# A banded Toeplitz matrix built on VectorE instead of by way of DRAM, and two input loads not tied to slots

## The chip, the cores and the metric

One core of one Trainium2 chip. The metric is the device time of one execution in microseconds (us). Medians of an execution series are given; where single executions matter they are listed. The record of each execution also holds the mean clock granted to TensorE.

## The reference, cut to what matters

A causal depthwise convolution with 7 taps per head, the taps normalised by a softmax, is followed by an RWKV channel mix:

```python
# x: (8, 4160, 192) float32; weight: (8 heads, 7 taps)
w = softmax(weight, axis=-1)
y[b, s, h, :] = sum_k w[h, k] * x_padded[b, s + k, h, :]      # 6 zeros in front
xk = mu_k * y + (1 - mu_k) * y_prev;  xr = mu_r * y + (1 - mu_r) * y_prev
k = relu(xk @ w_k);  v = (k * k) @ w_v;  r = sigmoid(xr @ w_r)
out = r * v
```

## The kernel before: the parts concerned

The convolution runs on TensorE (PE). Blocks of 128 rows of x are multiplied by a 128x128 banded "Toe" matrix per head, which yields 120 new rows. x comes in 18 groups of blocks; three buffers hold them. The first four groups are transposed on PE; the others go through DRAM (`y_write`, then a transposing DMA load `y_read`). Group numbers below are the code's (what the recorded texts call groups 5 and 6 are numbers 4 and 5); "conv 4" is the convolution of group 4.

```python
def x_tile(g, eng):
    xb = three.tile([P, GB, 2, D], BF16, tag="xb", name="xb")
    if blk0 == 0:
        eng.memset(xb[0:32, 0, :, :], 0.0)
    elif g > 3:
        eng.memset(xb[0:1, 0, 0, 0:2], 0.0)      # ties the load to this point of VectorE's queue
    if blk0 + nb == NBLK:
        eng.memset(xb[:, nb - 1, :, :], 0.0)
...
def load_toe():        # w_row: the taps, zero-padded, written to DRAM as w_scr before this
    nc.gpsimd.dma_start(out=toe, in_=bass.AP(tensor=w_scr.tensor, offset=w_scr.offset + K - 1,
                                             ap=[[H * P - 1, P], [P, H], [1, P]]))
...
def y_read(g):         # issued on SyncE's queue (SP)
    nc.sync.dma_start_transpose(out=yTs[p][:, :, YC + r0 : YC + r1], in_=y_drams[p][r0:r1, :])
...
def warm(n):           # filler: keeps PE busy so that its clock rises
    ps = psV.tile([P, BANK], FP32, tag="v", name="warm")
    for _ in range(n):
        nc.tensor.matmul(out=ps, lhsT=ones_t, rhs=zeros, start=True, stop=True)
...
# prologue, in order
load_x(0); warm(WARM); softmax()
nc.sync.dma_start(out=w_scr, in_=w_row); load_toe()
load_x(1); load_wk(); load_x(2); load_wr(); load_wv()
# convolution of group 0, warm(2), transposes, warm(5), convolution of group 1, warm(3), x_tile(3), load_x(3), main loop
```

## Time and profile before

| | kernel before |
|---|---|
| time, median (range) | 458.6 us (458.35 to 459.82), 3 executions |
| span of the profiled execution | 456.8 us |
| PE busy | 444.2 us, 97% |
| first convolution matmul | 11.77 us |
| first convolution matmul of group 4 | 36.67 us, behind a wait of 1.62 us for data |
| PE idle, 0 to 50 us / 50 to 400 us | 8.4 us / 0 us |

The prediction shows the lines.

### The profile page before, as it was taken

The numbers are of one execution on the slowest core, as the hardware profiler recorded it, in microseconds if no ns is written. First come the engines' busy times: TensorE is split into PE (matmuls) and PEld (weight loads), VectorE is DVE, ScalarE is ACT, GpSimd is POOL, SyncE is SP. The second block draws the span as 40 slices with busy tenths as digits, with TensorE's granted clock in tenths as the row PEclk, the third lists the DMA queues.
The fourth block names the chain that finished last, engine by engine and source line by source line (L and its number), as shares of the span: only waits on it lengthen the run. The fifth ranks groups of instructions, "written<-read, shape, count | busy, mean of one in ns | idle before, by whom it ended". The sixth has DMA issues, their size and how long they took to land.

```text
span 456.8 us, 10049 instructions
## 1 busy us (share of the span) xinstructions
PE 444.2 (97%) x3958; PEld 303.3 (66%) x3958; DVE 383.0 (84%) x759; ACT 355.8 (78%) x464; POOL 48.7 (11%) x69
## 2 busy tenths in 40 slices
PE   8877999999999999999999999999999999999996
PEld 3544676676777667767767677667676676666676
DVE  2598789887998888897998998987998997988963
ACT  2677987888888688888888788888887877767771
POOL 5742001102030010101020010100200000000000
PEclk9999999999999999999999999999999999999999
DMA  4999696899679794955859695778655563411223
GB/s 75 164 104 201 127 234 137 148 193 184 160 144 188 194 151 123 155 137 143 158 128 186 154 193 126 132 133 189 118 135 152 140 151 95 108 63 60 71 70 96
DMA packets 134402, 64.18 MB, mean 141 GB/s; under 512 B 85747, under 2 KB 133907, under 8 KB 134355
## 3 DMA queue, kind: packets, MB, share of 16 engines
q1 hardware_dynamic: 96050, 48.60, 42.7%
q0 software_dynamic: 38304, 14.95, 28.9%
q8 instruction: 31, 0.51, 0.4%
q14 instruction: 17, 0.13, 0.1%
HBM read 29.65 MB, written 37.25 MB: 146 GB/s over the span
## 4 chain that ended last, share of the span: by engine, by line
PE 94%; DVE 2%; DMA 2%; ACT 1%; issue 1%; POOL 0%; DVEq 0%
PE ps_k L348 39%; PE ps_v L454 37%; PE ps_r L431 5%; PE ps_r L432 5%; PE ps_c L205 4%; PE warm L556 3%; DMA xb<-in_x_dram 2%; PE ps_k L374 1%; DVE yT L274 1%; DVE xr L329 0%; PE ps_t L263 0%; DVE xr L326 0%; DVE k L405 0%; DVE d L287 0%; ACT r_sb L438 0%
## 5 line engine op out<-in xcount | busy, mean ns | idle before, releaser
L386 ACT ACTIVATE k_sb<-ps_k 128x1024 bf16<-128x1024 f32 x260 | 248.2, 1025 | 56.4 <-PE ps_k L348 52.2
L348 PE MATMUL ps_k<-xk,wk 128*128 128x512 bf16 (+3 forms) x1056 | 199.3, 374 | 0.5 <-ACT k_sb L386 0.4
L454 PE MATMUL ps_v<-wv,k 128*128 128x192 bf16 x2048 | 195.0, 246 | 1.9 <-DVE k L405 1.0
L454 PEld LDWEIGHTS <-k 128*128 128x128 bf16 x2048 | 172.8, 98 | 25.8 <-DVE k L405 1.2
L405 DVE TENSOR_TENSOR k<-k_sb 128x1024 bf16<-128x1024 bf16 x256 | 172.4, 684 | 4.5 <-ACT k_sb L386 4.3
L348 PEld LDWEIGHTS <-wk 128*128 128x128 bf16 (+1 forms) x1056 | 63.0, 96 | 104.7 <-issue 72.8
L467 DVE TENSOR_TENSOR o_sb<-ps_v,r_sb 128x384 f32<-128x384 f32 x128 | 70.9, 554 | 43.5 <-PE ps_v L454 42.8
L438 ACT ACTIVATE r_sb<-ps_r 128x768 bf16<-128x768 f32 x64 | 52.8, 825 | 15.9 <-PE ps_r L432 13.8
L225 ACT CAST y<-ps_c 120x480 bf16<-120x480 f32 (+5 forms) x85 | 39.7, 527 | 16.1 <-PE ps_c L205 16.1
L112 POOL DMA_DIRECT2D xb<-in_x_dram x36 | 32.5, 908 | 154.2 <-PE ps_k L348 67.5
L431 PE MATMUL ps_r<-wr,xr 128*128 128x192 bf16 x256 | 47.5, 246 | 1.2 <-DVE xr L329 1.0
L432 PE MATMUL ps_r<-wr,xr 128*128 128x192 bf16 x256 | 47.4, 246 | 0.3 <-DVE xr L329 0.3
L329 DVE TENSOR_TENSOR xr<-xr,yT 128x1024 bf16<-128x1024 bf16 (+1 forms) x66 | 36.3, 549 | 2.3
L329 DVE TENSOR_TENSOR xk<-xk,yT 128x1024 bf16<-128x1024 bf16 (+1 forms) x66 | 36.2, 549 | 2.3
L205 PE MATMUL ps_c<-xb,toe 128*128 128x480 bf16 (+4 forms) x144 | 31.8, 321 | 1.9 <-DMA xb<-in_x_dram 1.6
L287 DVE TENSOR_TENSOR d<-yT 128x1536 bf16<-128x1536 bf16 (+2 forms) x37 | 31.6, 853 | 1.5 <-DMA yT<-y_dram 1.5
L326 DVE TENSOR_SCALAR xk<-d,mu 128x1024 bf16<-128x1024 bf16 (+1 forms) x66 | 27.6, 418 | 0.2
L326 DVE TENSOR_SCALAR xr<-d,mu 128x1024 bf16<-128x1024 bf16 (+1 forms) x66 | 27.4, 414 | 0.0
L432 PEld LDWEIGHTS <-xr 128*128 128x128 bf16 x256 | 25.0, 98 | 2.3 <-issue 1.7
L431 PEld LDWEIGHTS <-xr 128*128 128x128 bf16 x256 | 25.0, 98 | 1.8 <-DVE xr L329 1.2
L228 ACT CAST y<-ps_c 120x480 bf16<-120x480 f32 (+7 forms) x47 | 21.5, 509 | 0.8 <-DVE yT L233 0.6
L556 PE MATMUL warm<-zeros,ones_t 128*128 128x512 bf16 x46 | 13.2, 446 | 1.9 <-DVE zeros L565 1.4
(51 smaller groups left out, 84.0 us busy)
## 6 DMA issues: line engine op xcount, KB each, us to landing
out_dram<-o_sb SPq DMA_DIRECT2D x128, 192.0 KB, 2.5
y_dram<-y SPq DMA_DIRECT2D x10, 900.0 KB, 6.7
xb<-in_x_dram POOLq DMA_DIRECT2D x14, 480.0 KB, 7.9
xb<-in_x_dram POOLq DMA_DIRECT2D x6, 432.0 KB, 9.7
xb<-in_x_dram POOLq DMA_DIRECT2D x10, 192.0 KB, 5.0
y_dram<-y SPq DMA_DIRECT2D x3, 450.0 KB, 4.1
y_dram<-y SPq DMA_DIRECT2D x1, 810.0 KB, 6.4
xb<-in_x_dram POOLq DMA_DIRECT2D x2, 384.0 KB, 9.8
```

What stands on the lines that cost most here:

```text
L205: nc.tensor.matmul(out=ps[:, :, :, i * G : (i + 1) * G], lhsT=toe[:, h, :], rhs=xbs[g][:, :nb, :, h * G : (h + 1) * G], start=True, stop=True,
L225: copy(out=yh[:, :, :, c0 : c0 + n], in_=ps[:BLK, :, :, 0:n])
L326: nc.vector.tensor_scalar(out=o, in0=d[:, sl, :L], scalar1=mu[:, i, part : part + 1], scalar2=None, op0=ALU.mult)
L329: nc.vector.tensor_tensor(out=o, in0=o, in1=yT[:, sl, c0 : c0 + L], op=ALU.add)
L348: nc.tensor.matmul(out=ps[:, i, f * L : (f + 1) * L], lhsT=wk[r, 0 if hi else 1, fs], rhs=xk[r, i if hi else 2, :L], start=start and f == ...
L386: nc.scalar.activation(out=k_sb, in_=ps.rearrange("p a b -> p (a b)"), func=AF.Relu)
L405: nc.vector.tensor_tensor(out=o, in0=i, in1=i, op=ALU.mult)
L431: nc.tensor.matmul(out=o, lhsT=hi, rhs=wr[:, 0, :], start=True, stop=False)
L432: nc.tensor.matmul(out=o, lhsT=lo, rhs=wlo, start=False, stop=True)
L438: nc.scalar.activation(out=r_sb, in_=ps[:, :, 0 : 2 * D], func=AF.Sigmoid)
L454: nc.tensor.matmul(out=o, lhsT=k2[:, f, t * P : (t + 1) * P], rhs=wv[:, f, :], start=(f == 0), stop=(f == NF - 1),)
L467: nc.vector.tensor_tensor(out=o_sb[:, :n, :], in0=v_ps.pop(m)[:, :n, :], in1=r_sbs.pop(m)[:, :n, :], op=ALU.mult)
```

## The change

The intent: the Toe matrix no longer goes to DRAM and back. Along a row it is periodic with period 8 inside its band, so VectorE makes it as (pattern of period 8) x (band mask). `mod8` is a mask of "column mod 8 equals row mod 8", made from the identity; `w_all` is the product of taps and shifted masks; a sum over the taps gives the pattern `w_per`; two masked products write `toe`. The matrix being ready sooner, 16 of the 36 warm-up matmuls go. Second part: groups 4 and 5 lose the small memset that tied their loads to a slot.

```diff
-    WARM = 36
+    WARM = 20
...
-        elif g > 3:
+        elif g > 5:
             eng.memset(xb[0:1, 0, 0, 0:2], 0.0)
...
-    def load_toe(): ...
+    def masks_mod8():                       # twice, into the halves of mod8
+        nc.vector.tensor_reduce(out=mod8[:, 8 * i : 8 * i + 8],
+            in_=ident.rearrange("p (c r) -> p r c", r=8), axis=mybir.AxisListType.X, op=ALU.add)
+    def masks_band(): ...                   # two affine_selects on GpSimd
+    def make_toe():
+        nc.vector.tensor_tensor(out=w_all, in0=w_nrm.unsqueeze(3).to_broadcast([P, H, K, 8]),
+            in1=bass.AP(tensor=m.tensor, offset=m.offset, ap=[m.ap[0], [0, H], [1, K], [1, 8]]), op=ALU.mult)
+        nc.vector.tensor_reduce(out=w_per, in_=w_all.rearrange("p h k r -> p h r k"),
+            axis=mybir.AxisListType.X, op=ALU.add)
+        for h0, h1 in ((0, 3), (3, H)):
+            nc.vector.tensor_tensor(out=toe[:, h0:h1, :] ..., in0=w_per ..., in1=band ..., op=ALU.mult)
...
         nc.vector.memset(ones_t, 1.0)
+        x_tile(0, nc.vector)
         nc.vector.memset(zeros, 0.0)
... (ident now ahead of load_x(0), the band mask after it)
         softmax()
-        nc.sync.dma_start(out=w_scr, in_=w_row)
-        load_toe()
+        make_toe()
         load_x(1)
```

More of the change, by code (lines that the diff above doesn't have):

```diff
@@ L129 @@
     ident = const.tile([P, P], BF16)
-    w_row = const.tile([P, H, P], BF16)
-    w_scr = dram.tile([P, H, P], BF16)
+    w_nrm = const.tile([P, H, K], FP32)
+    mod8 = const.tile([P, 16], FP32)
+    w_all = const.tile([P, H, K, 8], FP32)
+    w_per = const.tile([P, H, 8], BF16)
+    band = const.tile([P, P], BF16)
     toe = const.tile([P, H, P], BF16)
@@ L169, in softmax @@
         nc.vector.tensor_tensor(
-            out=w_row[:, :, 0:K],
-            in0=w_exp[:, :, ::-1],
+            out=w_nrm,
+            in0=w_exp,
             in1=w_sum.unsqueeze(2).to_broadcast([P, H, K]),
@@ L174, in softmax, with masks_band @@
         )
-    def load_toe():
-        nc.gpsimd.dma_start(
-            out=toe,
-            in_=bass.AP(
-                tensor=w_scr.tensor,
-                offset=w_scr.offset + K - 1,
-                ap=[[H * P - 1, P], [P, H], [1, P]],
-            ),
-        )
+    def masks_mod8():
+        for i in range(2):
+            nc.vector.tensor_reduce(
+                out=mod8[:, 8 * i : 8 * i + 8],
+                in_=ident.rearrange("p (c r) -> p r c", r=8),
+                axis=mybir.AxisListType.X,
+                op=ALU.add,
+            )
+    def masks_band():
+        nc.gpsimd.affine_select(
+            out=band, in_=ones_t, pattern=[[-1, P]], compare_op=ALU.is_ge, fill=0.0, base=0, channel_multiplier=1
+        )
+        nc.gpsimd.affine_select(
+            out=band, in_=band, pattern=[[1, P]], compare_op=ALU.is_ge, fill=0.0, base=K - 1, channel_multiplier=-1
+        )
+    def make_toe():
+        m = mod8[:, :]
+        nc.vector.tensor_tensor(
+            out=w_all,
+            in0=w_nrm.unsqueeze(3).to_broadcast([P, H, K, 8]),
+            in1=bass.AP(tensor=m.tensor, offset=m.offset, ap=[m.ap[0], [0, H], [1, K], [1, 8]]),
+            op=ALU.mult,
+        )
+        with nc.allow_low_precision(reason="a sum of one number and zeros"):
+            nc.vector.tensor_reduce(
+                out=w_per,
+                in_=w_all.rearrange("p h k r -> p h r k"),
+                axis=mybir.AxisListType.X,
+                op=ALU.add,
+            )
+        for h0, h1 in ((0, 3), (3, H)):
+            n = h1 - h0
+            nc.vector.tensor_tensor(
+                out=toe[:, h0:h1, :].rearrange("p h (c r) -> p h c r", r=8),
+                in0=w_per[:, h0:h1, :].unsqueeze(2).to_broadcast([P, n, P // 8, 8]),
+                in1=band.rearrange("p (c r) -> p c r", r=8).unsqueeze(1).to_broadcast([P, n, P // 8, 8]),
+                op=ALU.mult,
+            )
     ys, yTs, y_drams = {}, {}, {}
@@ L564, in prologue @@
         nc.vector.memset(ones_t, 1.0)
+        x_tile(0, nc.vector)
         nc.vector.memset(zeros, 0.0)
-        x_tile(0, nc.vector)
-        x_tile(1, nc.vector)
-        x_tile(2, nc.vector)
-        nc.vector.memset(w_row, 0.0)
-        nc.vector.memset(wr[:, 2:4, :], 0.0)
-        load_x(0)
         nc.gpsimd.affine_select(
@@ L580, in prologue @@
         )
+        load_x(0)
+        masks_band()
         warm(WARM)
+        x_tile(1, nc.vector)
+        x_tile(2, nc.vector)
+        masks_mod8()
+        nc.vector.memset(wr[:, 2:4, :], 0.0)
         softmax()
-        nc.sync.dma_start(out=w_scr, in_=w_row)
-        load_toe()
+        make_toe()
         load_x(1)
```

## The prediction

> **What bounds the kernel now.** I read the page first, for the budget of each engine:
>
> ```profile
> span 456.8 us, 10049 instructions
> ...
> PE 444.2 (97%) x3958; PEld 303.3 (66%) x3958; DVE 383.0 (84%) x759; ACT 355.8 (78%) x464; POOL 48.7 (11%) x69
> ```
>
> PE idles for only 456.8 - 444.2 = 12.6 us, so a change that leaves the matmuls of the main loop alone must take its gain from those idle pieces, or from PE work that is there only to pass the time (the warm-up matmuls). The sums over stretches say where the idle is:
>
> ```profile
> 0.00:12.00 12.00, 10.61 (x40) 4.43 (x41) 2.38 (x10) 3.02 (x4) 6.88 (x16) 1.00 0.47 75
> 12.00:22.00 10.00, 8.64 (x87) 5.71 (x85) 5.58 (x14) 6.36 (x16) 7.80 (x13) 1.00 1.36 172
> 22.00:50.00 28.00, 22.33 (x181) 13.26 (x180) 25.92 (x55) 22.23 (x33) 7.93 (x10) 1.00 1.12 141
> 50.00:100.00 50.00, 50.00 (x439) 33.52 (x436) 41.60 (x81) 41.89 (x57) 3.77 (x4) 1.00 0.86 172
> ```
>
> The columns are the stretch and its length, then busy time of PE, PEld, DVE, ACT, POOL. From 50 us on PE is full, and the same view has 100.00 of 100.00 up to 400 us. Between 22 and 50 us PE misses 5.67 us, and DVE is the full engine (25.92 of 28). The change can therefore act only before 50 us; whatever the start gains there, the PE-bound rest passes on one for one. The chain of work that ended last, in order of time, names the two large early pieces:
>
> ```profile
> 1.39 10.54 PE warm L556 x36
> ...
> 11.94 0.39 PE ps_c L205 x6
> ...
> 28.86 7.68 DMA xb<-in_x_dram
> 36.54 0.14 issue
> 36.67 0.56 PE ps_c L205 x2
> ```
>
> The first is filler, so I ask the timeline what it fills for:
>
> ```profile
> 5.28 0.22 DVE L169 TENSOR_TENSOR w_row<-w_exp,w_sum 128x56 bf16<-128x56 f32 x1
> 5.53 0.33 SPq L584 DMA_DIRECT2D w_scr<-w_row  x1
> ...
> 6.81 4.63 PEld L556 LDWEIGHTS <-ones_t 128*128 128x128 bf16 x22 [0.19 <-issue]
> ...
> 8.34 0.59 POOL L177 DMA_DIRECT2D toe<-w_scr  x1 [3.39 <-DMA w_scr<-w_row]
> 8.93 1.49 POOL L112 DMA_DIRECT2D xb<-in_x_dram  x2
> ...
> 11.59 0.66 PEld L205 LDWEIGHTS <-toe 128*128 128x128 bf16 x8
> 11.77 0.66 PE L205 MATMUL ps_c<-xb,toe 128*128 128x144 bf16 x8
> ```
>
> The taps are ready at 5.28 + 0.22 = 5.50. The Toe matrix goes to DRAM and back: 2.5 us to land, then an issue at 8.34 that lands 3.2 us later, 11.54. Its first weight load is at 11.59, while the last warm-up matmul ends at about 11.77. So 36 matmuls were tuned to the round trip; filler and round trip end together, and removing only one of them gains almost nothing. POOL also stands behind the round trip: the loads of x group 1 wait for it until 8.93.
>
> **What the Trainium skill says.** "DMA: Bandwidth & Descriptors", section "Anatomy of one DMA — SWDGE (gpsimd) path", gives a transfer a fixed part of about 2.0 us. The trace agrees: 2.5 and 3.2 us for the two legs. "TensorE: Matmul & The Clock Gate", Part 1, says that the cold array runs at half clock, that the release depends on a free-running window of activity and not on a number of matmuls, and that an N=512 matmul then takes about 216 ns instead of 427. The trace agrees: weight loads of the warm-up stand 0.43 apart up to 6.47, and from 6.81 on 22 take 4.63 us (21 steps of 0.216); the granted-clock column says 1.00 throughout, so it doesn't show this. "VectorE: DVE Perf Modes", section "The TRN2 errata", gives (N+151)/0.96 ns for an fp32 tensor_tensor, and its perf-mode tier table one element per cycle for tensor_reduce, two for a bf16 tensor_tensor. For the 56-element multiply above the formula gives 216 ns, the trace 0.22; for the bf16 128x1024 square (512+151)/0.96 = 691, the page 684.
>
> **The change part by part.**
>
> Removed on the start path: the two DMA legs, and 16 warm-up matmuls. All 16 are warm ones: 16 x 0.216 = 3.46 us. But the zeros that the warm-up reads are now set after the x tile's memset, which takes a pitch of about 0.26 us, so PE begins at 1.65 instead of 1.39. If the clock rises at the same absolute time, about 6.72 (part way through the matmul that begins at 6.47), (6.72 - 1.65)/0.427 = 11.9 matmuls run cold, the other 8.1 take 1.75, and the warm-up ends at 8.47. If it rises 0.26 later, 8.73. Against 11.77 that is 3.0 to 3.3 us; I take 3.2.
>
> Added on DVE after 5.50: w_all, 448 fp32 elements, (448+151)/0.96 = 0.62; w_per, a reduction of 448 elements, 0.62; the masked product for heads 0 to 2, 384 bf16 elements, 0.36 at two per cycle (0.56 at one); for the other five, 640 elements, 0.49 (0.82). With some 0.03 between, the first heads are ready at 7.2 and all at 7.7 (7.4 and 8.3 if the broadcast pattern falls to one per cycle). Both are before 8.47, so this lies beside the warm-up. Ahead of the softmax DVE gets two 128-element reductions, 0.29 each, after the identity mask; they and the other memset end by about 2.8, and the softmax can't begin before the weights land at 4.0 (the first DVE reduction starts at 4.02). Hidden. On POOL ident moves ahead of the x loads and the band adds two selects of 0.31 (ident's duration) after them: band by about 5.1, used at about 6.8. Hidden too. x group 0 landed at 7.4 before and its issues move by about -0.1: in time for 8.5.
>
> Moved: loads of x group 1 are issued at about 5.15 instead of 8.93, 3.8 us earlier, and everything in POOL's queue behind them (first weights, x group 2, the second layer's weights, x group 3) likewise. Since PE moves by 3.2, the loads keep up. What follows conv 0 (casts, transposes, five more warm-ups) is a chain of latencies that I carry over unchanged.
>
> The second part: the two L94 memsets that tie the loads of groups 5 and 6 to the DVE queue (group numbers 4 and 5 in the code) go. Now look at the load of the first of them:
>
> ```profile
> 27.30 0.06 DVE L94 MEMSET xb<- 1x1 uint32 x2
> 27.39 0.22 DVE L96 MEMSET xb<- 128x192 uint32 x1
> ...
> 27.92 1.89 POOL L112 DMA_DIRECT2D xb<-in_x_dram  x2 [6.51 <-PE ps_k L348]
> ...
> 36.67 0.56 PE L205 MATMUL ps_c<-xb,toe 128*128 128x480 bf16 x2 [1.62 <-DMA xb<-in_x_dram]
> ...
> 37.59 0.53 DVE L274 COPY yT<-ps_t 128x720 bf16<-128x720 bf16 x1 [1.63 <-PE ps_t L263]
> ```
>
> POOL sat idle for 6.51 us; the wait is put down to PE, but the issue follows the DVE memset. The buffer itself (that of group 1) was free when conv 1 ended at about 16.9. Freed, this load follows x group 3 directly, at about 21.4 - 3.8 = 17.6. Behind group 3, which landed at about 26.5, it needs some 5.1 us (its second half landed 2.5 us after the first), so it lands near 26.5 - 3.5 + 5.1 = 28. PE wants it at (36.67 - 1.62) - 3.2 = 31.9. The wait vanishes with almost 4 us to spare: PE gets 1.62 us back and DVE, the full engine of this stage, its 1.63; I count them once, 1.6, and 0.1 for the memsets. For the other group, the last of its pair of sequences, the memset L96 stays on DVE, so its load remains tied. That costs nothing: its convolution comes at slot 14, after 50 us, and the load used to land by 43.
>
> Sum: 3.2 + 1.6 + 0.1 = 4.9. 458.6 - 4.9 = 453.7 us, 1.1% less.
>
> **The rivals.** (a) The front becomes bound by loads. x group 2 landed at about 19.6 and conv 2 began at 19.69: no slack there. If the earlier loads, now running beside the tail of group 0, win only 2.5 us and not 3.8, the start gains 2.5 and the time is 454.4. For it: the DMA engines run without a break from 10 to 26 us. Against it: between 8 and 10 us they are at 0.12, so there is idle time for the loads to move into. (b) DVE becomes the bound: the product reads a broadcast operand and slows to one per cycle or worse, and the Toe matrix is ready only at 9.5. Then the start gains 2.3: 454.6. Against it: even the slow estimate, 8.3, is under the warm-up's end. (c) The wait for group 4's data goes, but DVE, at 1.97 of each 2 us from 24 to 34, is replaced by another wait: the gain is the front alone, 455.4. Against it: DVE itself was idle in that wait. (d) The shorter warm-up ends before the clock is up, or PE cools again. 20 matmuls last 6.8 us by the estimate and the clock needed 5.3; run by run the moment moves. If all 20 ran cold, they would end at 1.65 + 8.54 = 10.2 and the gain be 1.7 less: 455.4.
>
> **Range and chances.** The rivals together lose at most about 3 us and I see hardly a mechanism for more than 1 us extra (a stall in 22 to 34 us that shrinks). So 452.4 to 455.8. Faster by over 2% means under 449.4, which would need 9.2 us out of an early stage that has 8.4 us of PE idle and 3.5 us of removed filler: 2%. Slower by over 2%: 1%. Within 2%: 97%.
>
> **What would show it.** Right: first conv matmul at 8.4 to 8.8 straight behind the warm-up; Toe products done by 7.7; first load of x group 1 issued near 5.2; load of group 4 issued at 17 to 19 and no DMA wait of PE near 32; PE full from about 45 us on. Wrong: an idle PE between warm-up and first convolution (Toe or x late), a wait of conv 1, of the first layer or of conv 2 for a load, DVE idle with another releaser between 20 and 45 us, or matmuls of 427 ns after 8 us.

## The result, and the profile after

454.68 us median (454.34 to 455.03, 4 executions) against 458.86 (458.35 to 459.82, 4 executions): ratio 0.9906, 95% interval 0.9887 to 0.9926. Ratios here are the mean time of one kernel's fast runs over that of the other's of the same rounds, so not quite the ratio of the medians quoted. The class is "same" (within 2%), the predicted 453.7 is 1.0 us low, and the range 452.4 to 455.8 holds. The profiled execution has a span of 453.3 us, 3.5 less than before.

The sums over the same stretches as in the prediction, for the changed kernel (stretch, length, busy PE, PEld, DVE, ACT, POOL):

```profile
0.00:12.00 12.00, 9.06 (x41) 4.00 (x42) 6.25 (x20) 4.08 (x7) 10.01 (x21) 1.00 0.82 93
12.00:22.00 10.00, 8.73 (x90) 6.12 (x89) 7.44 (x18) 7.68 (x15) 6.62 (x9) 1.00 1.31 148
22.00:50.00 28.00, 25.50 (x203) 15.37 (x202) 26.14 (x52) 24.82 (x40) 5.96 (x8) 1.00 1.12 159
50.00:100.00 50.00, 48.68 (x429) 32.88 (x428) 41.34 (x81) 40.53 (x53) 3.77 (x4) 1.00 0.92 168
```

Between 22 and 50 us PE has 25.50 instead of 22.33 us of work: the stage runs better. But from 50 to 100 us, where PE was full, it now misses 1.32 us. The timeline of the changed kernel, at the start and around conv 4:

```profile
6.41 0.95 DVE L206 TENSOR_REDUCE w_per<-w_all 128x64 bf16<-128x448 f32 x1
7.47 0.76 DVE L214 TENSOR_TENSOR toe<-w_per,band 128x384 bf16<-128x384 bf16 x2
8.25 0.68 PEld L240 LDWEIGHTS <-toe 128*128 128x128 bf16 x8
8.45 0.66 PE L240 MATMUL ps_c<-xb,toe 128*128 128x144 bf16 x8
...
24.72 0.57 PE L240 MATMUL ps_c<-xb,toe 128*128 128x240 bf16 x4 [0.81 <-DMA xb<-in_x_dram]
...
31.31 0.57 PE L240 MATMUL ps_c<-xb,toe 128*128 128x480 bf16 x2
```

The first convolution is at 8.45, 3.32 us earlier. Conv 4 is at 31.31, 5.36 us earlier and without its wait. A wait of 0.81 us at conv 3 is new. It does no lasting harm: the next convolution, 26.75 here and 30.24 before, is 3.49 earlier. So 5.36 us were won by 31 us, and 3.5 are left at the end. The chain of work that ended last, in order of time, names the place; the pieces from 40 to 60 us of the changed kernel:

```profile
43.25 6.68 DMA y_dram<-y
49.94 0.02 issue
49.95 7.71 DMA yT<-y_dram
57.67 0.02 issue
57.69 0.96 DVE d L322
```

This is the round trip of group 4's convolution result: written to DRAM, read back by the transposing load, then used by VectorE. The write begins 5.24 us earlier than before (48.49), but the load lands at 57.66, only 3.24 earlier than before (60.90). The load took 7.71 us from issue to landing, not 5.85. In SyncE's queue the issuing instruction itself is longer; the kernel before, then the changed one:

```profile
55.05 3.81 SPq L248 DMA_TRANSPOSE yT<-y_dram  x1
```

```profile
49.95 5.70 SPq L283 DMA_TRANSPOSE yT<-y_dram  x1
```

and VectorE waits for it, before and after:

```profile
60.92 0.96 DVE L287 TENSOR_TENSOR d<-yT 128x1536 bf16<-128x1536 bf16 x1 [1.48 <-DMA yT<-y_dram]
```

```profile
57.69 0.96 DVE L322 TENSOR_TENSOR d<-yT 128x1536 bf16<-128x1536 bf16 x1 [3.49 <-DMA yT<-y_dram]
```

In steps of 1 us, the changed kernel's DMA engines during that issue (last two columns: mean busy DMA share, which counts a packet's whole time where it begins and can exceed 1, and GB/s):

```profile
52.00:53.00 1.00, 1.00 (x14) 0.95 (x12) 0.51 (x1) 1.00 (x2) 0.00 (x0) 1.00 3.38 188
53.00:54.00 1.00, 1.00 (x12) 0.85 (x10) 0.95 (x2) 1.00 (x3) 0.00 (x0) 1.00 0.00 0
54.00:55.00 1.00, 1.00 (x7) 0.31 (x6) 0.20 (x1) 0.45 (x2) 0.00 (x0) 1.00 0.20 38
55.00:56.00 1.00, 1.00 (x8) 0.31 (x5) 0.00 (x0) 0.74 (x1) 0.00 (x0) 1.00 1.28 290
```

In the middle of the transfer no byte moves for over a microsecond. In the trace's list of DMA packets, a 16 KB packet of kind "instruction" begins at 52.59, on queue 8, just ahead of this pause. There are 31 of these, and PE has 7,884 instructions in the changed kernel (the page's 3942 matmuls and as many weight loads): 31 blocks of 256 hold 7,936. The Trainium skill, "Runtime: NRT & Kernel Launch", section "Instruction fetch mechanics", says that each engine's instructions are streamed in 16 KiB blocks of 256 and that the cost of a block boundary is "mostly hidden". The trace agrees with the block size; c2 below, with 8,140 PE instructions, has 32 such packets. In the kernel before, the corresponding fetch began at 54.52, half a microsecond before the issue.

**Theory A.** A fetch of PE's instruction stream that meets the transposing load stalls it by 1 to 2 us. Its place shifted because the change takes 16 matmuls and 16 weight loads out of PE's stream. **Theory B**, the rival: y's round trip is simply exposed once PE comes earlier; the stall has nothing to do with the fetch. Other questions are whether start and loads each earn what was predicted, and why the reduction took 0.95 us.

### The profile page after: what moved, and what is told of

It reads as the page before. It is cut to its first block, busy times and chain, and to the rows that moved or that the text cites. A ratio compares the mean times of both kernels' runs of the same rounds, so it can differ in the third digit from the quotient of the medians.

```text
span 453.3 us, 10019 instructions
## 1 busy us (share of the span) xinstructions
PE 441.0 (97%) x3942; PEld 301.8 (67%) x3942; DVE 385.1 (85%) x762; ACT 355.8 (78%) x464; POOL 48.6 (11%) x70
## 4 chain that ended last, share of the span: by engine, by line
PE 87%; DVE 8%; DMA 3%; ACT 1%; issue 1%; DVEq 0%
PE ps_k L383 36%; PE ps_v L489 35%; PE ps_r L466 4%; PE ps_r L467 4%; PE ps_c L240 4%; DVE k L440 3%; PE warm L591 2%; DMA yT<-y_dram 2%; DMA y_dram<-y 1%; DVE d L322 1%; DVE yT L309 1%; PE ps_k L409 1%; DVE o_sb L502 1%; DVE xk L364 1%; DVE xr L361 1%
## 5 line engine op out<-in xcount | busy, mean ns | idle before, releaser
L240 PEld LDWEIGHTS <-toe 128*128 128x128 bf16 x144 | 12.7, 98 | 2.2 <-issue 1.5
```

Source lines behind the costliest of these rows:

```text
L240: nc.tensor.matmul(out=ps[:, :, :, i * G : (i + 1) * G], lhsT=toe[:, h, :], rhs=xbs[g][:, :nb, :, h * G : (h + 1) * G], start=True, stop=True,
```

## The experiments

Twelve kernels; all gave the reference's output. "At full clock" means executions with a mean granted clock of 0.998 or more; why they are separated appears in the text. (By the clock records of the traces, a fall to half clock lasts 3.413 us, which takes 0.0037 off the mean over 457 us. The last microseconds of an execution can be at half clock too: a3's last 2.1 us take off 0.0024. So 0.994 to 0.996 stands, by estimate, for one such fall on the way, and 0.993 or less for two.) The last three columns are from each kernel's profiled execution and concern group 4's transposing load; the fetch's place is its start less the start of the issue.

| run | median us (executions) | before, same call | at full clock: mean us (how many), less before's | fetch | issue us | DVE waits for yT |
|---|---|---|---|---|---|---|
| a1_again | 454.49 (6) | 458.37 | 454.45 (5), -3.6 | +2.84 | 5.09 | 2.69 |
| a2_start_only | 456.96 (6) | 458.37 | 456.30 (3), -1.8 | +2.68 | 5.21 | 2.84 |
| a3_loads_only | 456.11 (6) | 458.37 | 456.36 (6), -1.7 | -0.69 | 3.87 | 1.55 |
| a4_fetch_shift | 453.50 (5) | 458.37 | 453.34 (5), -4.8 | +0.18 | 3.75 | 1.63 |
| b1_before_fetch_in | 458.87 (6) | 459.19 | 458.60 (4), +0.2 | missed | 3.91 | 1.62 |
| b2_after_warm36 | 456.41 (4) | 459.19 | 456.56 (4), -1.8 | -0.60 | 3.83 | 1.51 |
| b3_before_warm20 | 460.94 (4) | 459.19 | 459.61 (1), +1.2 | +2.99 | 5.32 | 2.97 |
| b4_dense_reduce | 453.19 (4) | 459.19 | 453.18 (4), -5.2 | -0.77 | 3.59 | 1.30 |
| c1_fetch_half | 453.27 (4) | 458.75 | 453.41 (4), -5.2 | +1.25 | 4.45 | 2.26 |
| c2_before_fetch_in2 | 460.33 (6) | 458.75 | 459.87 (3), +1.3 | +2.43 | 5.16 | 2.79 |
| c3_start_only_shift | 456.40 (6) | 458.75 | 455.09 (2), -3.5 | -0.74 | 3.85 | 1.67 |
| d1_before_fill | 458.28 (5) | 459.47 | 458.26 (5), -0.3 | -0.13 | 4.07 | 1.80 |

The kernel before at full clock: 458.09 (6 of 11 executions), 458.37 (6 of 11), 458.61 (7 of 11), 458.60 (2 of 9) in the four calls.

**a1_again**: no edit.

> The changed kernel once more, for its spread and to see which details of its trace come back. Both theories: 454.2 to 455.0 us. Theory A (chance of place: a fetch of PE's instruction stream, one 16 KB block of 256 instructions, falls into the issue of the transposing load yT<-y_dram of group 5 and stalls it) expects that it comes back in the same place: the issue takes 5.5 to 6 us on the SP queue, DVE waits 3.3 to 3.7 us for yT. Theory B (the round trip of group 5's y through DRAM is simply exposed once PE comes earlier) expects the same DVE wait, but has no reason for an issue of 5.7 us instead of 3.8; if this issue comes back at 3.8 us with the same time, A falls.

454.49 us, ratio 0.991. The stall came back in the same place, a little smaller than expected (issue 5.09 us and not 5.5 or more, DVE's wait 2.69 and not 3.3 or more).

**a2_start_only**: the change without its second part.

```diff
-        elif g > 5:
+        elif g > 3:
```

> Only the start is changed; both loads stay tied to DVE by their memsets. The front gains 3.3 us (first convolution at 8.45 instead of 11.77) and the 1.62 us wait of conv 4 for its data is back. Theory A: PE has the same instruction count as the changed kernel, so the fetch comes at the same instruction, but y's round trip begins later by about 1.9 us on PE's clock; if it misses the issue the time is 458.7 - 3.3 = 455.4, if it hits 456 to 457. Theory B (the time after 50 us is set by the round trip of y): the y write begins at 45.2 and the gain is 3.3 us, 455.4, with DVE's wait for yT at 1.5 as in the kernel before.

Ratio 0.996, in A's "if it hits" band; the fetch hit (+2.68) and the issue took 5.21 us. The first convolution was at 8.43 and conv 4 waited 1.39 us. The start, alone, had seemed worth 3.3 us and gave 1.4 by the medians.

**a3_loads_only**: the kernel before with the two memsets gone.

```diff
-        elif g > 3:
+        elif g > 5:
```

> The kernel before with only the two memsets L94 taken out. The 1.62 us wait of PE for xb goes, y's write begins near 46.6 instead of 48.49. PE's instruction count is that of before. Theory A: the stall of the transposing load depends on where the fetch falls; before it fell 0.5 us ahead of the issue, now the issue is 1.9 us earlier while the fetch moves with PE, so it may fall just behind its start or ahead of it; without a hit the full 1.9 us are gained, 456.8. Theory B: y's round trip takes back most of it, DVE waits over 2.5 us for yT with an issue of 3.8 us, 457.5 to 458.5.

Ratio 0.9948. No stall, and 1.7 us at full clock against the predicted 1.7: 1.6 for the wait and 0.1 for the memsets. B's take-back is not there: DVE waits 1.55 us for yT, as before.

**a4_fetch_shift**: the changed kernel, with PE's instruction count brought back to 7,916 at the same warm-up time.

```diff
-        for _ in range(n):
-            nc.tensor.matmul(out=ps, lhsT=ones_t, rhs=zeros, start=True, stop=True)
+        for i in range(n):
+            for c in range(3 if n == WARM and i >= 12 else 1):
+                w = 168 if n == WARM and i >= 12 else BANK
+                nc.tensor.matmul(out=ps[:, 0:w], lhsT=ones_t, rhs=zeros[:, 0:w], start=True, stop=True)
```

> The changed kernel, where the last 8 warm-up matmuls of 512 columns become 24 of 168: same warm-up time within 0.1 us, but 16 matmuls and 16 weight loads more, so PE's instruction count is that of the kernel before and every fetch comes 32 instructions earlier in the program, some 1.3 to 1.7 us earlier on the clock. Theory A: the fetch now falls at about 51, still inside the issue (49.95 to 53.8) or at its start, so either the stall moves or, if the fetch comes before 49.95, it is gone: issue 3.8 us, DVE's wait for yT 1.6, time 453.0 to 453.5. Theory B: no effect, 454.7. If the fetch is seen inside the issue and the issue still takes 3.8 us, A falls.

453.50 us, ratio 0.9882. All five executions (452.95 to 453.60) lie below all six of a1 (454.15 and more). The issue of the same transposing load, in a4:

```profile
49.64 3.75 SPq L283 DMA_TRANSPOSE yT<-y_dram  x1
```

Only 32 harmless PE instructions differ, and B expected nothing. But the fetch began 0.18 us inside the issue, where by the words on record A should have fallen. A has to be narrowed: in a4 no packet begins between 0.2 and 1.4 us of the issue (the load's own packets, of 256 bytes, start 1.43 us in), and the fetch, 0.93 us long, was over by then. What seems to matter is whether the fetch meets the flow of the load's packets, not the issue. The second transposing load fits the narrowed form: nominally 3.2 to 3.7 us, it took 3.96, 4.61, 4.63, 5.39 and (in c2) 4.48 with a fetch 0.71, 0.23, 0.24, 0.35 and 0.41 us after its start; these fetches last until 1.4 to 2.0 us, so to the start of its own packets (about 1.4) or beyond.

All 14 traces together say more. Nine of an execution's 14 transposing loads have issues of nominally 3.6 to 4.1 us. The 11 of these issues with a fetch 2.3 to 3.0 us after their start took 5.03 to 5.70 us; of the 88 with no fetch beside them 83 took at most 4.3, and five 4.5 to 5.0. But the narrowed form is not the whole rule. At the fifth load (changed kernel, a1, a2, c2) fetches that began within 0.1 us of its start and were over by 1.35 us still held its packets back, to 2.4 us or later instead of 1.4, and the issue took 4.6 to 4.8 us. And the third load, with a fetch 0.35 to 0.52 us after its start, took 6.0 to 7.0 us, hardly more than the 5.6 to 6.9 of the executions without. Why a4's early fetch cost nothing is therefore not fully shown.

**b1_before_fetch_in**: the kernel before with its warm-up matmuls cut in three.

```diff
-        for _ in range(n):
-            nc.tensor.matmul(out=ps, lhsT=ones_t, rhs=zeros, start=True, stop=True)
+        for _ in range(n * 3 if n == WARM else n):
+            w = 170 if n == WARM else BANK
+            nc.tensor.matmul(out=ps[:, 0:w], lhsT=ones_t, rhs=zeros[:, 0:w], start=True, stop=True)
```

> The kernel BEFORE, with each of its 36 warm-up matmuls of 512 columns cut into three of 170: the same warm-up time within 0.1 us, 144 PE instructions more. The fetches of PE's stream then come 144 instructions earlier in the program; at the 2.8 us per 32 instructions seen between a1 and a4, less the 0.3 that PE itself moved, that is about 11 us: the one at 68.5 us comes near 57.5, 2.4 us into the issue of the transposing load (55.05 to 58.86). Theory A (a fetch amid the issue stalls it): the issue takes 5.0 to 5.8 us instead of 3.8, DVE waits 2.5 to 3.5 us for yT instead of 1.5, and the kernel before gets slower by 0.7 to 1.5 us, 459.0 to 459.9. Theory B (the exposed round trip of y): nothing moves earlier, no effect, 458.4. If the fetch lands elsewhere by its record, the run tells nothing of A.

The fetches moved by 7.5 us, not 11, and missed this load; time unchanged. It says nothing of the disputed load, but is a control: cutting the warm-up alone changes nothing. Two later transposing loads of the same execution did get a fetch 2.6 to 2.7 us into the issue, and took 5.49 and 5.41 us where other executions without such a fetch mostly had 3.7 to 4.1. Those are not waited for.

**b2_after_warm36** and **b3_before_warm20**: each matrix with the other's filler.

```diff
-    WARM = 20        # b2, the changed kernel
+    WARM = 36
-    WARM = 36        # b3, the kernel before
+    WARM = 20
```

> The changed kernel with the 36 warm-up matmuls of before. If the gain at the start is only the filler that the VectorE matrix lets go, the first convolution begins at 8.45 + 16 x 0.216 = 11.9 and the start gains nothing; PE's instruction count is that of before, so by A no stall: 458.4 + 0.2 - 2.0 (loads) = 456.6 us. If having the matrix and the x loads early were worth something by itself, less: under 455.5.

456.41 us: the matrix made on VectorE, with the old filler, is worth nothing at the start. What remains is the gain of the loads (a3).

> The kernel before, with the Toe matrix by way of DRAM, and 20 warm-up matmuls. The matrix lands at 11.54, so the first convolution begins at 11.6 instead of 11.77: a gain of 0.2 at most; PE then stands idle for 3.2 us from 8.3. If the clock falls in that pause, the following matmuls run at half rate and the loss is 1 to 2 us. PE has 32 instructions fewer, so by A the stall of the transposing load may appear here too: 458.2 without it, 459 to 460 with it. Whatever comes, over 455 us: the filler alone isn't the gain.

460.94 us, slower than before (1.0039, interval 1.0009 to 1.0070) and above the band. PE's timeline in b3:

```profile
11.02 0.67 PE L205 MATMUL ps_c<-xb,toe 128*128 128x144 bf16 x8 [2.49 <-DMA toe<-w_scr]
...
14.30 2.29 PE L556 MATMUL warm<-zeros,ones_t 128*128 128x512 bf16 x5 [0.41 <-DVE yT L274]
```

PE waits for the matrix, its clock falls (five filler matmuls take 2.29 us and not 1.24), and the fetch stalls the load as well. Neither half of the first part is a gain by itself.

**b4_dense_reduce**: a4 with `w_all` stored so that the reduction reads neighbours.

```diff
-    w_all = const.tile([P, H, K, 8], FP32)
+    w_all = const.tile([P, H, 8, K], FP32)
-            out=w_all,
+            out=w_all.rearrange("p h r k -> p h k r"),
-                in_=w_all.rearrange("p h k r -> p h r k"),
+                in_=w_all,
```

> a4 with w_all laid out so that the reduction to w_per reads neighbours instead of every eighth fp32 number (the product writes with the stride instead). The predicted 0.62 us for this reduction measured 0.95. If the stride of the read costs it, it falls to 0.6 to 0.7 here; if it is a cost for each of the 64 outputs, it stays at 0.9 to 1.0, and the product shows no change at 0.62. The time is that of a4 within 0.4, 453.1 to 453.9, since the warm-up ends after the matrix anyhow.

The same two instructions, in b4:

```profile
5.75 0.95 DVE L199 TENSOR_TENSOR w_all<-w_nrm,mod 128x448 f32<-128x448 f32 x1
6.74 0.62 DVE L206 TENSOR_REDUCE w_per<-w_all 128x64 bf16<-128x448 f32 x1
```

The reduction falls to the predicted 0.62, but the product, which now writes with a stride, rises from 0.62 to 0.95. So the 0.33 us belong to whichever instruction takes steps of 28 or 32 bytes through fp32 numbers, not to the reduction or its outputs. That fits the Trainium skill, "SBUF — State Buffer", section "Door 1: The DMA port swizzle", whose note has lines of 16 bytes and a penalty for accesses that don't hit a line twice. Time as in a4, as expected.

**c1_fetch_half**: a4 with the last 8 matmuls cut in two and not in three, 16 instructions more than the changed kernel.

```diff
-            for c in range(3 if n == WARM and i >= 12 else 1):
-                w = 168 if n == WARM and i >= 12 else BANK
+            for c in range(2 if n == WARM and i >= 12 else 1):
+                w = 256 if n == WARM and i >= 12 else BANK
```

> The changed kernel with its last 8 warm-up matmuls of 512 columns cut in two (a4 cut them in three): 16 PE instructions more than the changed kernel, where a4 had 32. It is the control for a4: the warm-up is cut in the same way, but the fetch should fall at about 1.3 us after the start of the transposing issue (2.64 in the changed kernel, 0.18 in a4), so amid it. Theory A: the issue takes 4.3 to 5.3 us, DVE waits 2.0 to 3.0 us for yT, time 454.0 to 454.6. If the cutting itself made a4 faster, or if it was chance: issue 3.8 us, 453.5 us.

The fetch came at +1.25, the issue took 4.45 and DVE waited 2.26: the trace is as A has it. The time is not: 453.27 us, as in a4. A stall of about 0.65 us costs nothing that can be measured. PE's busy time from 50 to 70 us, in the changed kernel, in c1, and in b4 (no stall):

```profile
50.00:70.00 20.00, 18.68 (x167) 12.59 (x166) 14.28 (x27) 15.26 (x19) 0.00 (x0) 1.00 0.81 161
```

```profile
50.00:70.00 20.00, 19.75 (x174) 13.27 (x173) 15.47 (x29) 15.98 (x21) 0.00 (x0) 1.00 0.80 185
```

```profile
50.00:70.00 20.00, 20.00 (x177) 13.44 (x177) 16.19 (x31) 16.30 (x20) 0.00 (x0) 1.00 0.78 198
```

PE is idle for 1.32 us with the long stall, 0.25 with the short one and not at all without. Together with the stall of 1.3 to 1.9 us in the changed kernel, which costs 1.1, this suggests that PE has about half a microsecond of other work in store. By its time alone c1 can't exclude that the cut itself makes the changed kernel faster, as its expectation has it; against that stand PE's idle times above and b1, which was cut, had no stall and gained nothing.

**c2_before_fetch_in2**: the kernel before with 148 warm-up matmuls of 124 columns; the mirror of a4.

```diff
-        for _ in range(n):
-            nc.tensor.matmul(out=ps, lhsT=ones_t, rhs=zeros, start=True, stop=True)
+        for _ in range(148 if n == WARM else n):
+            w = 124 if n == WARM else BANK
+            nc.tensor.matmul(out=ps[:, 0:w], lhsT=ones_t, rhs=zeros[:, 0:w], start=True, stop=True)
```

> The kernel BEFORE with 148 warm-up matmuls of 124 columns instead of 36 of 512, in the same time within 0.2 us: 224 PE instructions more. Since a block is 256 instructions, that is as if there were 32 less than in the kernel before, which is the count of b3 modulo 256, where the fetch fell 2.99 us into the issue. b1 missed the issue; this should hit it at 2.5 to 3.2 us. Theory A: issue 5.0 to 5.8 us instead of 3.8, DVE waits 2.5 to 3.5 us for yT instead of 1.5, time 0.7 to 1.5 us over the kernel before of the same rounds. Otherwise: no change beyond 0.3 us.

The fetch hit, in the kernel before:

```profile
56.41 5.16 SPq L248 DMA_TRANSPOSE yT<-y_dram  x1
```

Ratio 1.0026 (1.0009 to 1.0043), 1.3 us slower at full clock: the same accident, put into the kernel before, costs it what it costs the changed one. But c2's profiled execution was already 1.36 us late at y's write, before the stall. Its 2 us sums, with the granted clock in the third column from the end:

```profile
34.00:36.00 2.00, 0.82 (x8) 0.59 (x7) 1.89 (x5) 0.86 (x1) 1.95 (x3) 1.00 1.60 190
36.00:38.00 2.00, 1.50 (x12) 1.29 (x13) 0.39 (x1) 0.90 (x2) 1.15 (x2) 0.76 1.61 192
38.00:40.00 2.00, 2.00 (x12) 1.36 (x10) 1.52 (x5) 0.14 (x2) 0.00 (x0) 0.50 1.50 208
```

PE's clock is halved, for 3.4 us by the clock record, from 37.05 us on, half a microsecond after conv 4's wait ended (eight matmuls of L454 take 1.49 us there and not 0.82). That is a third effect. Something of the kind was in the executions of the kernel before all along: of its 42 in these four calls, 21 have a mean clock of 0.995 or 0.994 and take 0.9 to 1.7 us longer (means, by call); 3.4 us at half clock cost at most 1.7. None of these was profiled, so where in them the clock fell is inferred. b3's profiled execution shows it too, at 0.50 from 38 to 40 us.

**c3_start_only_shift**: a4 without the second part of the change.

```diff
-        elif g > 5:
+        elif g > 3:
```

> a2 (only the start changed) with the cut of a4: PE's instruction count is that of before. Theory A: a2's issue of 5.2 us falls back to 3.8, and the start alone gains its 3.3 us: 455.0 to 455.5 where a2 had 456.96 against 458.37. If the start's gain is lost for another reason than the stall, it stays over 456.

The issue fell back to 3.85 us and DVE's wait to 1.67, as A has it. The median of 456.40 is over 456 all the same: four of its six executions are at a clock of 0.994 or lower. The two at full clock took 455.30 and 454.87, 3.5 us under the kernel before. Two executions are few; with a3's they fit the prediction's terms, 3.5 and 1.7.

**d1_before_fill**: filler into the wait, in the kernel before.

```diff
     def conv(g, c):
+        if g == 4 and c == 0:
+            warm(6)
         conv_mm(g, c)
```

> The kernel BEFORE with six warm-up matmuls put in front of the first convolution of group 5 (number 4 in the code), 6 x 0.216 = 1.3 us of filler into PE's 1.62 us wait for that group's data; the loads stay tied. It tests a third effect that the runs so far suggest: in 14 of 33 executions of the kernel before the mean granted clock is 0.994 or 0.995 and the time 1.4 us longer, and in the one profiled execution of that kind (c2) the half clock begins at that wait, for 3.4 us. Kernels with the loads freed show it in 1 of 30. If PE's idleness in that wait lets the clock fall, the filler cures it: every execution at a clock of 0.998 or more and at 457.8 to 459.0 us, median 458.3, spread under 1.2 us, beside runs of the kernel before of which some 2 in 5 are at 459.6 or more. If the loads act on the clock in another way, 2 or 3 of the 6 stay at 459.6 or more. PE has 12 instructions more, so the fetch comes a little ahead of where it was and misses the transposing issue as before.

All five executions were at 0.998 or more, at 457.93 to 458.48 us, while 7 of the 9 of the kernel before beside them were at 0.995 or 0.994. The 3.5 us around the wait, in the kernel before, in d1, and (the same stretch of the program) in the changed kernel:

```profile
33.50:37.00 3.50, 1.15 (x10) 0.81 (x10) 2.42 (x7) 1.40 (x2) 2.27 (x4) 1.00 1.59 192
```

```profile
33.50:37.00 3.50, 2.50 (x16) 1.48 (x17) 2.27 (x6) 1.24 (x2) 2.50 (x4) 1.00 1.60 192
```

```profile
29.50:33.00 3.50, 2.64 (x32) 2.08 (x30) 3.46 (x9) 2.93 (x5) 2.49 (x4) 1.00 1.50 172
```

PE is busy for 1.15 us of 3.5 in the first, 2.50 in the second (its filler) and 2.64 in the third (work). The Trainium skill, "TensorE: Matmul & The Clock Gate", Part 1, tells of a free-running window of 3413 ns after whose idleness the clock falls. The traces agree with the window: each half clock on the way lasts 3,413 ns, and the full clock between lasts whole multiples of it. They do not need an idle window, though. In c2 the window that ended as the clock fell ran from 33.64 to 37.05 us, and PE was busy for 1.37 us of it; in b3 it was 1.26 us. The profiled executions of the kernel before (first fence above) and of b1 did not fall; the window over the same wait has 1.58 and 1.67 us in them, and 2.63 in d1. So where the windows happen to lie against the wait decides, as far as these traces show; an exact threshold does not come out of them, since b3's clock also fell after a window with 1.72 us (from 10.22 us on) and not after the one before it, with 1.72 too.

The counts go the same way. Kernels with the loads freed (the first four executions of the changed kernel, a1, a3, a4, b2, b4, c1) show a clock under 0.998 in 1 execution of 33, and none of their profiled windows between the warm-up and 60 us has PE busy for less than about 2.0 us. The other kernels with the loads tied and no filler (a2, b1, b3, c2, c3) show it in 15 of 28.

## Why the prediction was right, and where it was off

**The bound, and the stretch where a gain is possible: right.** PE is full from 100 to 400 us in both kernels, and all differences arose before 100 us.

**The start, 3.2 us: right, measured 3.32** in the profile and 3.5 at full clock (c3, two executions). A single profile is good to some 0.4 us here: with 20 filler matmuls the first convolution began between 8.08 (a4) and 8.85 (c3), with the moment at which the clock rose (the clock record starts at 6.00 in the one and 7.58 in the other). b2 and b3 show that filler and round trip had to go together, as argued.

**The Toe matrix on DVE, ready at 7.7: too early, it was 8.23.** The reduction was mis-sized, 0.62 for 0.95 us, since its stride was overlooked; the softmax came 0.22 us later too, mainly because the weights landed at 4.14 and not at 4.0. It stayed hidden all the same: in a2 the matrix was ready at 7.91, and the first convolution began at 8.43, no earlier than with 8.23. But most of the margin that the prediction saw was gone.

**The loads keep up: nearly.** Group 3's last half landed at 24.59, 1.95 us earlier and not 3.5; PE waited 0.81 us at conv 3. Rival (a) showed itself there, without lasting cost, and not at conv 2. Rivals (b), (c) and (d) did not come: the matrix was ready at 8.23, a3 gained the 1.7 us of the wait, and the eight matmuls of the first convolution take 0.66 us as before.

**The wait of conv 4, 1.6 + 0.1: right.** From the first convolution to conv 4 it is 22.86 us instead of 24.90, 2.04 less, and a3 gained 1.7. The load was issued at 18.17 and 19.20 and landed at 29.7, not 28; PE came at 31.31.

**The sum: this step failed.** "From 50 us on PE is full ... whatever the start gains there, the PE-bound rest passes on one for one": it did not. 1.1 us (a1 against a4) were given back at the transposing load of group 4, by a stall of its packets that goes with the place of an instruction fetch, and that no rival named. The wait was in sight in the kernel before, 1.48 us long, and it was passed over (PE stood full beside it). Of the prediction's own signs, "PE full from about 45 us on" is the one that did not come: 48.68 of the 50 us from 50 to 100. Without the stall, the sum of 4.9 is met: a4 gains 4.8 at full clock, b4 5.2.

**Smaller readings.** Of the two DMA legs that the prediction holds against the Trainium skill's fixed part for the GpSimd path, only the second (3.2 us) goes by GpSimd; the first (2.5 us) was issued on SyncE's queue, of which that section does not speak.

**The baseline: not looked at.** 458.6 was taken as one number. It is two, 458.4 and 459.8 (means of 21 executions each), by whether the clock falls on the way (at conv 4's wait in c2 and b3, the two profiles that show it). The freed loads also end this, which the prediction did not count; at full clock the changed kernel gains 3.6 us (a1), and the recorded ratio, with slower executions among those of before, says 4.3 (0.94% of 458.86). Two misses, 1.1 us one way and some 0.7 the other, partly cancel in the recorded time. Being near the median was in part luck.

**What stays open.** How the fetch stalls the load is not shown. The two overlap in time, moving the fetch moves the stall, both ways and in either kernel, and hardly a byte moves during it; whether they meet in one DMA engine, in its rings or in SyncE's descriptors is not in the trace. That it is PE's stream rests on the block count (31, and 32 in c2) and on PE's instruction count being what moved it. Not every longer issue has a fetch beside it: five others stand at 4.5 to 5.0 us without one. And that conv 4's idleness makes the clock fall is shown by d1 (0 of 5 executions) and by the freed loads, but only two executions that fell there (c2, b3) were profiled.

The fastest versions are a4, c1 and b4, at 453.2 to 453.5 us. They beat both kernels, by the changed kernel plus a cut of its filler that does nothing but move the fetches. This will not survive the next edit of PE's stream.

## What to carry to other kernels

When filler and a latency end together, change both or neither, and check each alone. When a stage with a full engine is handed a head start, list the waits beside it that were just covered (here a DRAM round trip, 1.48 us) before assuming that the head start arrives whole. And when executions of one kernel fall into two groups a microsecond apart, read the granted clock of each: a short stretch with a mostly idle PE can cost more than its own length, and filling it is cheap.

## What the Trainium skill lacked or had wrong

- "Runtime: NRT & Kernel Launch", Instruction fetch mechanics, calls the cost of a block boundary mostly hidden. Here transposing loads with such a fetch 2.3 to 3.0 us after the start of their issue have issues of 5.0 to 5.7 us instead of 3.8, and the kernel loses 1.1 us (a1 against a4) or 1.3 us (c2).
- "DMA: Bandwidth & Descriptors", DMA Transpose (X-bar), does not mention it, and Queues, rings and completion order puts refill on row 14. If the trace's queue numbers are these rows, that is half of it: 16 instruction packets of 8 KB are on queue 14, but the 31 of 16 KB for an execution are on queue 8.
- "TensorE: Matmul & The Clock Gate", Why this matters for your kernels, advises against idle gaps over about 3 us. Here c2's clock fell after a window of 3.41 us in which PE was busy for 1.37 us and no gap was over 1.49; by the mean clock, half of the executions of the kernel before have such a fall. With 2.63 of 3.41 us (d1's profile) it did not fall, nor in d1's four other executions.
- "VectorE: DVE Perf Modes", The TRN2 errata: the formula (N+151)/0.96 holds for the dense 448-element fp32 operations (0.62 us measured, 0.62 by it) but not with steps of 28 or 32 bytes (0.95 us); the page doesn't say so, though the SBUF page's note on 16-byte lines leads there.
